# Attention and a cosine feed-forward: the output product of one more double tile done by seven block products

## The chip, the cores and the metric

The kernel runs on one core of one Trainium2 chip. The metric is the device time of one execution in microseconds (us). Before the change the median of three runs is 776.25 us (775.53 to 776.44).

The names of the engines in the profile: PE is TensorE's matmuls and PEld its weight loads, DVE is VectorE, ACT is ScalarE, POOL is GpSimd, SP is the queue that issues the DMAs.

## The reference

Attention within chunks of 64 positions, then a feed-forward layer with h·cos(h) between its two products, in fp32:

```python
scores = matmul(q_c, k_c^T) / sqrt(64)           # chunks of 64 of a sequence of 576; 8 batches, 8 heads
attn = softmax(scores); out = matmul(attn, v_c)
x = out.transpose(0, 2, 1, 3).reshape(4608, 512) # tokens by model width
h = x @ w_in                                     # w_in 512 x 2048
g = h * cos(h)
return g @ w_out                                 # w_out 2048 x 512
```

## The kernel before

Accuracy of fp32 is kept by splitting every operand into a high and a low fp32r part; a product is then three matmuls: high by high, high by low, low by high. In the profile the parts of g are `g_hi` and `g_lo`.

The 4608 tokens make 9 tiles of 512. Tiles 0 and 1 go first, alone. The other seven are handled in units: unit 0 is tile 2, unit 1 tiles 3 and 4, unit 2 tiles 5 and 6, unit 3 tiles 7 and 8. Attention of a later tile runs beside the feed-forward layer of an earlier unit.

**The hidden product** of a double tile is done by seven block products instead of eight (Strassen's scheme in Winograd's form): two halves of the tokens (the two tiles) by two halves of the hidden features. For each of eight pairs k of feature blocks there are seven products of six 128x512 matmuls (L324); sums of blocks of w_in are streamed from HBM. VectorE and ScalarE combine the seven results into four blocks of h (L969 copies, L972 additions) and make g out of each by four steps: an activation (`whole`, L975), `turn` (L978), an activation with the sine (`sine`, L982), and a multiplication (`times`, L985). Then g is split: a cast to g_hi (L339 on VectorE, L341 on ScalarE) and a subtraction to g_lo (L345 on VectorE or GpSimd).

**The output product** has two forms.

- Plain, `wide_pair` (L1610), in units 1 and 2: for each feature block of 128 and each 128 tokens three matmuls of 128x512. The first tile of the unit is multiplied at once, the g of the second tile is stored to the HBM tensor `gathered`, read back by `second_tile` (L1717) after the last pair, split and multiplied.
- By blocks, `block_pair` (L1775) and `block_products` (L1925), in unit 3: again seven products instead of eight, of 128x256 matmuls, over halves of the features, of the tokens and of the output columns. P1 and P2 take blocks of g as they are and run inside the pairs. For the other five, VectorE or GpSimd makes sums Z1 to Z4 of blocks of g (128x256 each, L345); these and the block Z22 are stored to the HBM tensor `sums` (L1897, L1899), and come back after the last pair, are split and multiplied with differences of w_out. Those differences are made by `differences_of_w` (L1690) during unit 1, stored to the HBM tensor `diffs` (L1711), loaded and split.

**Rooms.** Inside `block_pair` the four blocks of g of a pair lie in rooms in SBUF that the next pair takes again. In the last unit (`ends`) there are two rooms for each half of a pair (K_ROOMS, taken in turn: `twice = 2`), in another unit one (U_ROOM, T_ROOM: `twice = 1`). The first activation of a later pair, `w1`, waits for everything that reads the room (`k_users`, L1845, L1905): the store of Z22, the four sums and the split. In the last unit that is the pair before last, in another unit the pair before. The rooms of Z1 to Z4 (`q_room`, L1915) are the tiles of q and k in the last unit, else a tile of g, `half1` and the room `ds_room(1)`.

**What sets the order.** Every piece of work is appended with its engine and its dependences; then two tables decide. `RANK` gives each piece its place in one order, and so its place in its engine's queue; `ELSEWHERE` lists the pieces that run on their other engine (a split or a sum on GpSimd instead of VectorE). Engines work their queues strictly in order.

Of the kernel before, what the change touches and what calls it, by code (L numbers as in the profile page):

```python
# [289 lines left out]
def attention_then_cos_ffn(ctx: ExitStack, tc, qT, kT, v, w_in, w_out, out, wide):  # L290
# [593 lines left out]
    UNITS = 1 + (NT - FAST) // 2  # L884
# [133 lines left out]
    def out_part(t, fc, sub, half=None):  # L1018
# [15 lines left out]
        matmul(o, g_lo[:, ss], w_hi, start=False, stop=last, **on)  # L1034

    KK = NPAIR // 2
    BLOCKED = range(UNITS - 1, UNITS)
    ROWS, COLS = 2, HALF
    Z22, Z1, Z2, Z3, Z4 = range(5)
    V1, V3, V2, V4 = range(4)  # L1040
# [1456 lines left out]
```

## Time and profile before

| what | value |
|---|---|
| median of 3 runs | 776.25 us |
| the profiled execution | 775.76 us |
| its span | 774.1 us |
| TensorE matmul busy | 761.9 us, 98% |
| VectorE busy | 646.1 us, 83% |
| ScalarE busy | 444.6 us, 57% |
| GpSimd busy | 290.2 us, 37% |
| DMA, mean | 229 GB/s, 66.8% of 16 engines |

The profiled execution is one run; its span is the stretch from the first to the last recorded instruction, 1.66 us shorter than its device time. TensorE works nearly the whole span at a granted clock of 0.999 of full speed, so a reader looks for what shortens its work, and for what makes it wait.

The stages, as the timeline shows them: unit 2 (its pairs and its output product) from 457 to 621 us, the pairs of unit 3 from 621 to 707 us, the five products of unit 3 with the last results from 707 us on.

### The profile page before, as it was taken

Reading aid. Unit: us, or ns where it says so; the run is one execution under the profiler, and the core shown is the slowest. Engines: PE = TensorE matmul, PEld = TensorE weight load, DVE = VectorE, ACT = ScalarE, POOL = GpSimd, SP = SyncE. Lnnn points to the kernel's source line nnn. Section 1 sums busy time; section 2 is a strip of 40 time slices with the busy share of each in tenths; the row PEclk is TensorE's granted clock in tenths of the full one; section 3 lists DMA queues with packets and bytes.
Section 4 is the critical chain, followed back from the end, with each engine's and each line's share of the span. In section 5 each row is a group of like instructions: output and inputs, shape, how many; then the busy total and the mean of one; then the engine's idle time right before and its main releaser. Section 6 shows DMA issues by size and latency. Waiting matters only on the chain.

```text
span 774.1 us, 16060 instructions
## 1 busy us (share of the span) xinstructions
PE 761.9 (98%) x6100; PEld 676.2 (87%) x6100; DVE 646.1 (83%) x1100; ACT 444.6 (57%) x814; POOL 290.2 (37%) x261
## 2 busy tenths in 40 slices
PE   7999999999999999999999999999999999999997
PEld 6888888888999988888888888888888889989997
DVE  5997998889899987896899888777898667999983
ACT  6997885456884467555642445555443455556631
POOL 2442235968541344562521621201102027454144
PEclk9999999999999999999999999999999999999999
DMA  9995530389969645868674753757544376999973
GB/s 340 401 409 198 177 110 1 124 270 357 377 195 313 194 170 202 260 223 298 224 256 126 256 150 127 257 179 268 178 136 137 116 238 215 325 300 334 337 270 110
DMA packets 95756, 177.21 MB, mean 229 GB/s; under 512 B 9152, under 2 KB 39872, under 8 KB 95680
## 3 DMA queue, kind: packets, MB, share of 16 engines
q1 hardware_dynamic: 95680, 176.20, 66.8%
q8 instruction: 48, 0.79, 0.4%
q14 instruction: 28, 0.23, 0.1%
HBM read 127.93 MB, written 48.23 MB: 228 GB/s over the span
## 4 chain that ended last, share of the span: by engine, by line
PE 90%; DVE 4%; DMA 3%; POOL 1%; issue 1%; ACT 0%; SPq 0%; DVEq 0%; ACTq 0%
PE acc L324 41%; PE h L324 36%; PE a L324 13%; DVE g_lo L345 1%; DMA vt<-in_v_dram 1%; DMA w_in<-sums 1%; DMA sums<-qt 1%; POOL g_lo L345 1%; DMA kt<-in_kT_dram 1%; DVE g_hi L339 0%; DMA w_in<-diffs 0%; PE a L1207 0%; DVE x L345 0%; SPq L321 0%; DVE w_in L972 0%
## 5 line engine op out<-in xcount | busy, mean ns | idle before, releaser
L324 PE MATMUL acc<-w_out,g_hi 128*128 128x512 f32 (+1 forms) x976 | 278.3, 369 | 0.0
L324 PE MATMUL h<-x,w_in 128*128 128x512 f32 (+1 forms) x960 | 225.9, 364 | 0.0
L324 PEld LDWEIGHTS acc<-w_out,g_hi 128*128 128x128 f32 x976 | 178.1, 189 | 23.4 <-DVE w L339 0.7
L324 PEld LDWEIGHTS h<-x,w_in 128*128 128x128 f32 x960 | 171.2, 189 | 22.2
L324 PE MATMUL acc<-w_out,g_lo 128*128 128x512 f32 (+1 forms) x488 | 179.1, 367 | 0.0
L345 POOL TENSOR_TENSOR g_lo<-g,g_hi 128x512 fp32r<-128x512 f32 x38 | 53.2, 1400 | 193.2 <-ACT g_hi L341 97.9
L324 PEld LDWEIGHTS acc<-w_out,g_lo 128*128 128x128 f32 x488 | 92.4, 189 | 11.6
L324 PE MATMUL h<-w_in,w_in 128*128 128x512 f32 (+1 forms) x384 | 98.1, 354 | 0.5 <-DVE w_in L972 0.5
L324 PEld LDWEIGHTS h<-w_in,w_in 128*128 128x128 f32 x384 | 65.8, 190 | 8.7 <-DVE w_in L972 0.7
L982 ACT ACTIVATE w_in<-w_in 128x512 f32<-128x512 f32 x64 | 39.5, 628 | 18.8 <-DVE w_in L978 18.8
L341 ACT CAST g_hi<-g 128x512 fp32r<-128x512 f32 x52 | 32.0, 615 | 28.9 <-PE acc L324 8.5
L324 PE MATMUL a<-w_in,w_in 128*128 128x512 f32 (+1 forms) x204 | 42.5, 348 | 0.0
L345 DVE TENSOR_TENSOR g_lo<-g,g_hi 128x512 fp32r<-128x512 f32 x51 | 38.8, 761 | 3.2 <-ACT g_hi L341 2.5
L324 PE MATMUL a<-x,w_in 128*128 128x512 f32 (+1 forms) x192 | 41.2, 353 | 0.0
L345 POOL TENSOR_TENSOR g_lo<-w_in,g_hi 128x512 fp32r<-128x512 f32 x14 | 22.8, 1632 | 44.0 <-ACT g_hi L341 22.5
L324 PEld LDWEIGHTS a<-w_in,w_in 128*128 128x128 f32 x204 | 34.5, 190 | 4.0
L324 PEld LDWEIGHTS a<-x,w_in 128*128 128x128 f32 x192 | 33.2, 190 | 4.0
L969 ACT COPY a<-h 128x512 f32<-128x512 f32 x28 | 16.0, 571 | 33.5 <-PE h L324 31.0
L341 ACT CAST g_hi<-w_in 128x512 fp32r<-128x512 f32 x30 | 18.5, 619 | 26.1 <-PE acc L324 12.3
L345 DVE TENSOR_TENSOR g_lo<-w_in,g_hi 128x512 fp32r<-128x512 f32 x32 | 28.9, 916 | 5.2 <-ACT g_hi L341 4.9
L969 ACT COPY h<-h 128x512 f32<-128x512 f32 x28 | 16.0, 570 | 29.3 <-PE h L324 24.5
L725 ACT ACTIVATE g<-h 128x512 int32<-128x512 f32 x32 | 19.1, 596 | 23.4 <-PE h L324 20.7
(295 smaller groups left out, 1523.4 us busy)
## 6 DMA issues: line engine op xcount, KB each, us to landing
w_in<-combo SPq DMA_DIRECT2D x84, 512.0 KB, 4.8
combo<-w_in SPq DMA_DIRECT2D x56, 256.0 KB, 4.3
w_in<-combo SPq DMA_DIRECT2D x56, 256.0 KB, 5.3
qt<-in_qT_dram SPq DMA_DIRECT2D x36, 256.0 KB, 5.6
kt<-in_kT_dram SPq DMA_DIRECT2D x36, 256.0 KB, 5.6
w_in<-in_w_in_dram SPq DMA_DIRECT2D x16, 512.0 KB, 9.7
w_out<-in_w_out_dram SPq DMA_DIRECT2D x16, 512.0 KB, 9.9
gathered<-w_in SPq DMA_DIRECT2D x32, 256.0 KB, 3.1
```

The lines of the kernel that those rows point to most:

```text
L324: kept(nc.tensor.matmul(*args, **kw))
L341: kept(nc.scalar.copy(out=out, in_=in_))
L345: kept(eng.tensor_tensor(out, a, b, op=op))
L725: lambda: kept(nc.scalar.activation(n, h, AF.Identity, bias=0.25, scale=0.5 / math.pi)),
L969: kept(nc.scalar.copy(out=out, in_=in_))
L982: kept(nc.scalar.activation(g, g, AF.Sin, bias=0.5 * math.pi))
```

## The change

One number is changed in the code: the units whose output product goes by blocks start one earlier. The tables RANK (3206 numbers before, 3453 after) and ELSEWHERE are written anew for the whole kernel; of RANK two lines are shown.

```diff
 RANK = (
-    26, 32, 38, 44, 47, 37, 13, 56, 59, 64, 63, 53, 73, 78, 83, 75, 72, 81, 86, 90, 88, 79, 94, 98, 101, 99, 105,
...
+    3168, 3295, 3305, 3235, 3311, 3316, 3318, 3326, 3327, 3339, 3350, 3335, 3130, 3264, 3334, 3274, 3328, 3331,
...
-    BLOCKED = range(UNITS - 1, UNITS)
+    BLOCKED = range(UNITS - 2, UNITS)
```

So unit 2 (tiles 5 and 6) goes through `block_pair` and `block_products`, with `ends` false: one room a half, and the other rooms for the sums. The line that makes the differences of w_out, `if u == UNITS - 3` (L2431), is the same in both kernels. Lines of the changed kernel below the tables have numbers 15 higher.

Counted over the whole program, TensorE loses 384 matmuls of 128x512 and gets 672 of 128x256. VectorE gets 53 instructions more, ScalarE 39, GpSimd 49. The DMAs go from 574 to 654: 32 transfers of `gathered` fall away, 40 stores and 40 loads of `sums` and 16 loads of `diffs` are added, and results go out in more, smaller pieces.

TensorE's queue in a pair of unit 2 before: plain output products (`acc<-w_out,g_hi` and `g_lo`), and the start of a hidden block product (`h<-w_in,w_in`).

```order
L324 MATMUL acc_5902<-w_out_1122,g_hi 128x512 x2
L324 MATMUL acc_5902<-w_out_1122,g_lo 128x512
L324 MATMUL acc_5914<-w_out_997,g_hi 128x512 x2
L324 MATMUL acc_5914<-w_out_997,g_lo 128x512
L324 MATMUL h<-w_in_5449,w_in_6207 128x512
L324 MATMUL h<-w_in_5612,w_in_6207 128x512
L324 MATMUL h<-w_in_5449,w_in_6207 128x512 x2
L324 MATMUL h<-w_in_5612,w_in_6207 128x512
```

The same place of the changed kernel:

```order
L339 MATMUL acc_5932<-w_out_1033,g_hi 128x256 x2
L339 MATMUL acc_5932<-w_out_1033,g_lo 128x256
L339 MATMUL acc_5941<-w_out_1087,g_hi 128x256 x2
L339 MATMUL acc_5941<-w_out_1087,g_lo 128x256
L339 MATMUL acc_5941<-w_out_1087,g_hi 128x256 x2
L339 MATMUL acc_5941<-w_out_1087,g_lo 128x256
L339 MATMUL acc_5969<-w_out_1033,g_hi 128x256 x2
L339 MATMUL acc_5969<-w_out_1033,g_lo 128x256
L339 MATMUL acc_5932<-w_out_1033,g_hi 128x256 x2
L339 MATMUL acc_5932<-w_out_1033,g_lo 128x256
L339 MATMUL h<-w_in_5454,w_in_6289 128x512
```

The output matmuls of a pair are half as wide and belong to P1 and P2 alone; the rest of the output product stands in one run after the last pair.

VectorE's queue in a pair of unit 2 before, from a step of g to the next pair's additions (`L972`); the multiplications L985 end a block of g.

```order
L978 SCALAR_TENSOR_TENSOR g<-g,w_in_6149 128x512
L345 TENSOR_TENSOR g_lo<-g,g_hi 128x512
L985 TENSOR_TENSOR g<-w_in_6149,g 128x512
L339 CAST g_hi<-g 128x512
L642 STREAM_TRANSPOSE e_5754<-e_5792 32x8x32
L972 TENSOR_TENSOR w_in_6257<-a_6236,w_in_3870 128x512
L972 TENSOR_TENSOR w_in_6257<-h,w_in_3870 128x512
L978 SCALAR_TENSOR_TENSOR g<-g,h 128x512
L978 SCALAR_TENSOR_TENSOR g<-g,w_in_6257 128x512
```

And of the changed kernel, from the multiplication that ends the second block in one room (`w_in_6324`) to the first step in the next pair's block, which lies in the same room (`w_in_6541`); `g` and `w_in_3888` with 128x256 are the sums Z.

```order
L1000 TENSOR_TENSOR w_in_6324<-w_in_6344,w_in_6324 128x512
L1000 TENSOR_TENSOR w_in_6376<-w_in_6344,w_in_6376 128x512
L354 COPY e_5793<-a_6432 128x8x64
L354 COPY e_5793<-h 128x8x64
L360 TENSOR_TENSOR g<-g,w_in_6324 128x256
L360 TENSOR_TENSOR w_in_3888<-w_in_6376 128x256
L360 TENSOR_TENSOR g<-w_in_6324 128x256
L354 CAST g_hi<-w_in_6376 128x512
L354 COPY e_5752<-a_6389 128x8x64
L993 SCALAR_TENSOR_TENSOR w_in_6541<-w_in_6541,h 128x512
```

The sums stand between the steps of g, and between a block's last step and the next use of its room there are eight other instructions.

## Rows read from the trace of the kernel before

**Rows 1.** The page: the span, and each engine's busy time (part 1).

```profile
span 774.1 us, 16060 instructions
...
PE 761.9 (98%) x6100; PEld 676.2 (87%) x6100; DVE 646.1 (83%) x1100; ACT 444.6 (57%) x814; POOL 290.2 (37%) x261
```

**Rows 2.** Busy time by stretch, core 0; the head line names the columns.

```profile
core 0: us, PE busy (x) PEld busy (x) DVE busy (x) ACT busy (x) POOL busy (x), PEclk, DMA share, GB/s
457.00:621.00 164.00, 164.00 (x1232) 143.35 (x1231) 129.65 (x230) 80.41 (x133) 22.55 (x18) 1.00 0.52 176
621.00:707.00 86.00, 85.47 (x466) 76.43 (x465) 70.55 (x113) 47.88 (x84) 41.03 (x42) 1.00 0.85 277
707.00:747.00 40.00, 39.31 (x335) 38.21 (x335) 38.06 (x65) 21.63 (x39) 12.12 (x7) 1.00 0.98 331
...
260.00:280.00 20.00, 20.00 (x132) 18.61 (x131) 19.64 (x28) 11.75 (x23) 10.40 (x7) 1.00 0.73 235
```

**Rows 3.** The chain of waits, from 568 us: start, length, engine, what, line, instructions.

```profile
568.46 5.18 PE acc L324 x24
...
741.21 5.21 POOL g_lo L345
...
747.85 10.72 PE a L324 x96
```

**Rows 4.** Groups by line, VectorE, 621 to 707 us: busy us, mean ns, idle.

```profile
L978 DVE SCALAR_TENSOR_TENSOR w_in<-w_in,w_in 128x512 f32<-128x512 int32 x13 | 9.9, 772 | 0.3
...
L985 DVE TENSOR_TENSOR w_in<-w_in,w_in 128x512 f32<-128x512 f32 x13 | 9.5, 734 | 2.7 <-ACT w_in L982 2.6
...
L345 DVE TENSOR_TENSOR g_lo<-w_in,g_hi 128x512 fp32r<-128x512 f32 x8 | 9.3, 1192 | 1.3 <-ACT g_hi L341 1.3
...
L345 DVE TENSOR_TENSOR qt<-w_in 128x256 f32<-128x256 f32 x7 | 4.5, 647 | 0.0
...
L345 DVE TENSOR_TENSOR kt<-w_in 128x256 f32<-128x256 f32 x6 | 3.3, 544 | 0.0
...
L345 DVE TENSOR_TENSOR qt<-w_in,qt 128x256 f32<-128x256 f32 x2 | 0.8, 418 | 0.0
...
L345 DVE TENSOR_TENSOR g_lo<-g,g_hi 128x512 fp32r<-128x512 f32 x1 | 0.7, 684 | 0.0
```

**Rows 5.** The same view, GpSimd, 621 to 707 us.

```profile
L345 POOL TENSOR_TENSOR g_lo<-w_in,g_hi 128x512 fp32r<-128x512 f32 x6 | 8.7, 1450 | 6.6 <-DVE g_hi L339 6.6
...
L345 POOL TENSOR_TENSOR qt<-w_in 128x256 f32<-128x256 f32 x7 | 6.3, 904 | 11.9 <-DVE w_in L985 11.9
```

**Rows 6.** Timeline of VectorE: start, length, instruction; two stretches.

```profile
658.54 0.42 DVE L345 TENSOR_TENSOR kt<-w_in 128x256 f32<-128x256 f32 x1
658.88 1.23 DVE L978 SCALAR_TENSOR_TENSOR w_in<-w_in,w_in 128x512 f32<-128x512 int32 x1
...
709.32 0.68 DVE L345 TENSOR_TENSOR w_in<-w_in 128x512 fp32r<-128x512 f32 x1
709.92 0.68 DVE L345 TENSOR_TENSOR g_lo<-g,g_hi 128x512 fp32r<-128x512 f32 x1
```

**Rows 7.** Groups by line, VectorE, the whole span: transposes of the attention.

```profile
L642 DVE STREAM_TRANSPOSE pts<-e 32x256 f32<-32x256 f32 x40 | 17.0, 432 | 0.9
```

**Rows 8.** Line L1897, the 128 KB stores of unit 3's block of g.

```profile
L1897 SPq DMA_DIRECT2D sums<-w_in x16: 320/398/1027, 620.0 to 716.1; - x16
...
DMA to landing us min/median/max: 1.7/4.8/7.1
```

**Rows 9.** The DMA view: issues, KB each, median us to landing.

```profile
gathered<-w_in SPq DMA_DIRECT2D x32, 256.0 KB, 3.1
```

**Rows 10.** Timeline of TensorE at a late operand in unit 3's products.

```profile
737.63 0.38 PE L324 MATMUL acc<-x,g_lo 128*128 128x256 f32 x1 [0.24 <-DVE g_lo L345]
```

**Rows 11.** Tile diffs: its stores, with first and last start.

```profile
L1711 SPq DMA_DIRECT2D diffs<-w_in x16: 370/382/1457, 306.7 to 398.0; - x16
```

383 rows, old and new, of tables (ELSEWHERE, RANK) are left out of this document.

## The prediction

> **What bounds the kernel now.** I read the page first: TensorE's matmuls are busy 761.9 of 774.1 us, 98%, VectorE 83%, GpSimd 37% [rows 1]. So the time is TensorE's work, and a change must take work from it or make it wait. The table by stretch says where it waits: in unit 2, from 457 to 621 us, not at all (164.00 of 164.00) with VectorE busy 129.65 and DMAs at a share of 0.52; in unit 3, which already does its output product by blocks, 0.53 us in the 86 us of pairs and 0.69 in the 40 us of products [rows 2]. Unit 3 is therefore the nearest picture of what unit 2 becomes. What differs is shown nowhere in the trace: unit 2 also carries the attention of tile 7, and its pairs have one room for g where unit 3 has two. The chain of waits gives the prices of the two matmuls: 24 of 128x512 in 5.18 us, 0.2158 us each, and 96 of 128x256 in 10.72 us, 0.1117 each [rows 3]. The narrow one costs a little over half.
>
> **TensorE's work.** 384 x 0.2158 = 82.9 us goes, 672 x 0.1117 = 75.0 us comes: -7.8 us. That is the only term that can make the kernel faster, and as TensorE never waits in unit 2, it counts in full if nothing else is late.
>
> **VectorE in the pairs.** I add up the changed queue between the first addition of pair 0 and that of pair 7. TensorE's matmuls there make 97.1 us by the two prices above. VectorE has 163 instructions. They follow one another closer than their length: 0.60 us from start to start where the row says 0.68, 0.34 where it says 0.42 [rows 6]. So 108 on 512 elements x 0.60 = 64.8, 31 transposes x 0.43 [rows 7] = 13.3, 16 on 256 elements or casts x 0.34 = 5.4, 8 tiny ones x 0.2 = 1.6 (my estimate): 85.1 us. To this comes what GpSimd does to VectorE. In unit 3's pairs VectorE's instructions with two operands in SBUF are longer than the 684 ns (512 elements) and 418 ns (256 elements) of undisturbed ones: 13 x 88, 13 x 50, 8 x 508, 7 x 229 and 6 x 126 ns, 8.2 us together [rows 4], beside 41.03 us of GpSimd's work [rows 2], 0.20 us for each. In the changed queue GpSimd has 42 sums x 0.904 and 13 splits x 1.450 [rows 5], 56.8 us, in these pairs: +11.4. VectorE then needs 96.5 of 97.1 us. TensorE kept its pace with VectorE at 19.64 of 20 us, 98% [rows 2], so 96.5 / 0.98 = 98.5, +1.4 us.
>
> **The single room.** The first activation in a room waits for the store of Z22 of the pair before. In the changed queue of VectorE the time from the end of a block's last step to the first step in its room's next block is, by the same durations, 11.97, 6.82, 5.40, 4.72, 3.76, 9.14 and 6.49 us over the seven pairs; the excerpt of the changed queue shows the one of 3.76. In it must fit the issue (0.4, rounded to 0.5) and landing of the store and the activation with its signals (0.7, my estimate). Landing took 4.8 us in the median and 7.1 at most in unit 3, at a DMA share of 0.85 [rows 2, 8], and 3.1 in the stretches of `gathered`, at 0.52 and with twice the bytes [rows 2, 9]. At 3.1 only one pair is late, by 0.5 us; at 4.8 three are, 0.6 + 1.3 + 2.2 = 4.1; at 7.1 five are, some 14 us. The changed pairs move about what unit 3's do (277 GB/s x 86 us = 23.8 MB) in 97 us, 246 GB/s, so I put the share at 0.76 and the landing at 4.3 us: 2.6 us late. Part of this VectorE makes up, as the other pairs have 2 to 7 us to spare, and part is the same idle time as the 2% above. For the pairs I take +2.5 us together, between 0.5 and 7 (4.1 and twice 1.4).
>
> **The products of unit 2.** TensorE's work there is 67.5 us. VectorE has 122 instructions: 86 x 0.60 + 17 x 0.43 + 19 x 0.34 = 65.4, and 11 splits on GpSimd x 1.450 x 0.20 = 3.2, 68.6 us. 68.6 / 0.98 = 70.0, +2.5. Beside it operands come late as in unit 3, where a matmul waited 0.24 us for a split [rows 10] and a split on GpSimd of 5.21 us stood in the chain [rows 3]; that stretch lost 0.69 us in 40, so 1.2 in 67.5. They overlap with the first; I take +3.0, between 1.2 (VectorE ahead by its pieces done early) and 7.4 (both, and as much again, since here every split starts from a load). The loads themselves: 40 of `sums`, 16 of `diffs`, the streamed w_in, q, k, v and the results make some 20 MB in 67.5 us, 300 GB/s, where unit 3's products had 331 at a share of 0.98 [rows 2]; they fit, with little to spare. The differences are no new work: their stores ran from 306.7 to 398.0 us [rows 11], before unit 2 begins, and the order has them at the same place.
>
> **The rest.** ScalarE gets 39 instructions of about 0.6 us, 23 us on an engine with 57% [rows 1]: hidden by VectorE's queue, which is longer; in the products it has some 48 us of 67.5. SP issues 80 more DMAs, 0.4 us each [rows 8], 32 us over two stretches of 165 us: hidden, though a store now queues behind the streams, which is in the 0.5 us above. Unit 3's pairs and products keep their code. The order before unit 2 is rewritten too, with 12 VectorE instructions more ahead of unit 0's first addition; TensorE's idle time outside the stretches above is 12.2 - 1.2 = 11.0 us, nearly all at the start and the end, and I let it move by 0, at most 1.5 either way.
>
> **The sum.** -7.8 + 2.5 + 3.0 + 0 = -2.3 us on the profiled execution's 775.76 (its span 774.1 and 1.66 around it), 773.45. That execution lies 0.49 us under the median of the runs, so 773.9 us.
>
> **Rivals.**
>
> A. The whole saving arrives. For it: TensorE lost nothing with VectorE at 98%, and unit 3 does the same work with 0.53 us lost [rows 2]. Against it: there VectorE had 18% to spare. It needs landings near 3.1 us. -7.8 + 0.5 = -7.3 to -7.8: 768.5 to 769.0.
>
> B. VectorE takes TensorE's place as the bound and the time stays. VectorE's 96.5 + 68.6 = 165.1 us stand against 172.4 (164.6 and the 7.8 saved): the change is worth nothing from the point where VectorE can't be kept busy more than 95.8%. The trace has 38.06 of 40 with a loss and 19.64 of 20 without [rows 2], one on either side: 776.2, give or take 1.5.
>
> C. Slower, by the single room. If the landings of Z22 are 5.9 us, halfway between median and maximum of unit 3 [rows 8], the same list gives 0.3 + 1.7 + 2.4 + 3.3 + 0.6 = 8.3 us; with the products' 3.0 that is +3.5: 779.7. By itself it turns the sign from about 5.1 us of landing, where the list gives 5 us. For it speaks the DMA share, against it that unit 2 moves its bytes in more time.
>
> D. Slower, by GpSimd standing in VectorE's way more than in unit 3. If every us of GpSimd blocks VectorE for the share of its time that goes to instructions with two SBUF operands, 0.33 in the pairs and 0.67 in the products as I count the queue, VectorE needs 85.1 + 18.7 = 103.8 and 65.4 + 10.7 = 76.1, 179.9 us in place of 164.6: -7.8 + 15.3 = +7.5, 783.7. Against it: unit 3's 0.20 is what that overlap did cost, with a like mixture. The Trainium skill, "SBUF — State Buffer", section "Who interferes with whom", has this as a rule: VectorE and GpSimd share one pair of ports as an exclusive lock, so that "the other **fully blocks** (not throttle)". The trace agrees that splits beside GpSimd take 1192 ns in place of 684 [rows 4]; it does not show each of them blocked, so I keep the measured rate in the sum.
>
> **How the numbers follow.** What a measurement can tell from no change is 0.2%, 1.55 us. Forecast (part of the saving, 770 to 774.7): 0.42. A: 0.13. B (774.7 to 777.8): 0.22. C: 0.14, D: 0.09. So faster 0.55, same 0.22, slower 0.23. The forecast's own range is 770 to 774.7; to hold 8 in 10 it reaches down to A and up over C: 768.4 to 780.5.
>
> **What would show it.** In the changed profile: 672 more matmuls at 0.11 us and 384 fewer at 0.216; a stretch of some 100 us of pairs in unit 2 with TensorE idle 2 to 3 us in it, released by VectorE's L987; VectorE at 95% or more there; activations L990 of a first block waiting on DMA of `sums` in two or three pairs (C: in most of them, DMA as releaser, over 1 us each). In the products of unit 2 TensorE's gaps end with g_lo on VectorE or GpSimd. If VectorE's two-operand instructions average above 900 ns there, D is right. The prediction is wrong if TensorE loses time in unit 3 or before 457 us, which I cost at nothing, or if unit 2's loads land late enough that TensorE waits on a DMA.

## The result and the profile after

The changed kernel takes 786.41 us, median of 4 runs (785.79 to 787.93), the kernel before 776.35 us beside it: a ratio of 1.0127, with a 95% interval of 1.0112 to 1.0142. It is 10 us slower; the forecast was 773.9 us and its range ended at 780.5. (The section on the change says 3206 numbers for the table RANK before; it has 3216. It says 39 more instructions for ScalarE; the two profiles below differ by 53, of which 47 are casts, and by 31.8 us of ScalarE's time, where the prediction counted 23.)

The page of the changed kernel, span and part 1, answers to [rows 1]:

```profile
span 784.1 us, 16988 instructions
...
PE 760.1 (97%) x6388; PEld 678.0 (86%) x6388; DVE 678.0 (86%) x1153; ACT 476.4 (61%) x867; POOL 330.7 (42%) x310
```

The number of matmuls rose by 288 as counted, but their busy time fell by 1.8 us only and the time in which TensorE does nothing rose from 12.2 to 24.0 us. Measured from start to start (median 216 ns for 128x512, 112 for 128x256, and 109 and 7 for the small ones, which are the same in both kernels), TensorE's work fell by 7.7 us, as predicted, from 725.6 to 717.9. What grew is the rest of the time between its first and its last matmul, the time lost, from 40.0 to 58.1 us. Part of it counts as busy: after a wait the first group of matmuls is about 0.10 us longer, as in this row of TensorE's timeline in a pair of unit 2, where six take 1.56 us in place of 1.46 (start, length, instruction, the idle time before it and who ended it):

```profile
489.59 1.56 PE L339 MATMUL h<-w_in,w_in 128*128 128x512 f32 x6 [0.60 <-DVE w_in L987]
```

The table by stretch of the changed kernel (to be read beside [rows 2]; in this kernel unit 2's pairs run from about 452 to 558 us, and its products to 628, where unit 3's pairs take over):

```profile
core 0: us, PE busy (x) PEld busy (x) DVE busy (x) ACT busy (x) POOL busy (x), PEclk, DMA share, GB/s
0.00:452.00 452.00, 444.17 (x3842) 389.60 (x3843) 392.68 (x672) 285.21 (x537) 211.15 (x194) 1.00 0.68 237
452.00:556.00 104.00, 100.20 (x873) 86.82 (x872) 92.79 (x161) 62.48 (x102) 49.62 (x54) 1.00 0.74 246
556.00:600.00 44.00, 38.58 (x316) 36.57 (x316) 39.90 (x71) 28.64 (x51) 12.02 (x9) 1.00 1.02 358
600.00:640.00 40.00, 38.10 (x402) 35.98 (x401) 36.24 (x63) 21.63 (x39) 5.39 (x4) 1.00 0.51 168
```

Four things are to be seen. TensorE, which never waited in unit 2 before, is idle 3.8 us in the pairs, 5.4 in the first 44 us of the products and 1.9 around the step to unit 3. VectorE is busy 92.79 us of 104 in the pairs, 89%, which is less than the 95% that the prediction named. The DMAs are at a share of 1.02, busy all the time, and at 358 GB/s from 556 to 600 us, and at half of that afterwards. And before 452 us TensorE is busy 444.17 us, where the kernel before has

```profile
0.00:452.00 452.00, 445.54 (x3851) 391.61 (x3852) 391.67 (x673) 285.12 (x541) 203.95 (x187) 1.00 0.68 235
```

TensorE's waits from 452 to 636 us (in all, times, longest):

```profile
engine line waited for: us in total, times, longest us
PE h L339 <- DVE w_in L987: 2.2, 3, 1.4
PE h L339 <- DVE w_in L1000: 1.4, 2, 0.9
PE acc L339 <- ACT half L356: 1.2, 1, 1.2
PE a L339 <- DVE g_lo L360: 1.1, 2, 0.8
PE a L339 <- ACT g_hi L356: 1.0, 2, 0.6
PE h L339 <- ACT h L984: 0.7, 1, 0.7
PE acc L339 <- ACT w L356: 0.7, 1, 0.7
PE h L339 <- ACT e L356: 0.7, 1, 0.7
```

They have many releasers and none stands out: VectorE's additions (L987) and multiplications (L1000) in the pairs, casts of loaded sums and copies that empty banks of PSUM, TensorE's result memory, by ScalarE (L356) in the products. So the causes have to be left out one after the other.

### The profile page after: what moved, and what is told of

Same layout as the page of the kernel before. It is cut to its first block, busy times and chain, and to the rows that moved or that the text cites. A ratio compares the mean times of both kernels' runs of the same rounds, so it can differ in the third digit from the quotient of the medians.

```text
span 784.1 us, 16988 instructions
## 1 busy us (share of the span) xinstructions
PE 760.1 (97%) x6388; PEld 678.0 (86%) x6388; DVE 678.0 (86%) x1153; ACT 476.4 (61%) x867; POOL 330.7 (42%) x310
## 4 chain that ended last, share of the span: by engine, by line
PE 85%; DMA 6%; DVE 5%; ACT 2%; issue 1%; SPq 1%; DVEq 0%; ACTq 0%
PE acc L339 37%; PE h L339 32%; PE a L339 15%; DMA w_in<-combo 2%; DVE w_in L993 1%; DVE w_in L1000 1%; DMA x<-diffs 1%; SPq L336 1%; DMA qt<-in_qT_dram 1%; DMA x<-sums 1%; DMA w_in<-sums 1%; DVE w_in L987 1%; DMA kt<-in_kT_dram 1%; DVE g L360 0%; ACT w_in L990 0%
## 5 line engine op out<-in xcount | busy, mean ns | idle before, releaser
L339 PE MATMUL acc<-w_out,g_hi 128*128 128x512 f32 (+1 forms) x848 | 224.6, 352 | 0.0
L339 PEld LDWEIGHTS acc<-w_out,g_hi 128*128 128x128 f32 x848 | 150.6, 190 | 17.0
L339 PE MATMUL acc<-w_out,g_lo 128*128 128x512 f32 (+1 forms) x424 | 148.3, 350 | 0.0
L360 POOL TENSOR_TENSOR g_lo<-g,g_hi 128x512 fp32r<-128x512 f32 x33 | 44.4, 1345 | 123.2 <-ACT g_hi L356 81.2
L339 PEld LDWEIGHTS acc<-w_out,g_lo 128*128 128x128 f32 x424 | 80.5, 190 | 8.1
L360 POOL TENSOR_TENSOR g_lo<-w_in,g_hi 128x512 fp32r<-128x512 f32 x18 | 25.3, 1412 | 57.9 <-PE acc L339 24.7
L356 ACT CAST g_hi<-w_in 128x512 fp32r<-128x512 f32 x51 | 31.4, 620 | 23.3 <-PE acc L339 11.0
L360 DVE TENSOR_TENSOR g_lo<-w_in,g_hi 128x512 fp32r<-128x512 f32 x52 | 38.7, 753 | 6.0 <-ACT g_hi L356 5.4
L990 ACT ACTIVATE w_in<-w_in 128x512 int32<-128x512 f32 x40 | 25.0, 629 | 25.6 <-DVE w_in L987 24.8
L990 ACT ACTIVATE w_in<-h 128x512 int32<-128x512 f32 x40 | 23.9, 598 | 23.1 <-PE h L339 20.2
L993 DVE SCALAR_TENSOR_TENSOR w_in<-w_in,h 128x512 f32<-128x512 int32 x40 | 27.4, 685 | 11.5 <-ACT w_in L990 11.0
L360 POOL TENSOR_TENSOR w_in<-w_in 128x256 f32<-128x256 f32 (+1 forms) x31 | 27.3, 895 | 20.8 <-DMA x<-sums 12.5
L1000 DVE TENSOR_TENSOR w_in<-w_in,w_in 128x512 f32<-128x512 f32 x40 | 30.4, 763 | 2.5 <-ACT w_in L997 2.3
```

Source lines behind the costliest of these rows:

```text
L339: kept(nc.tensor.matmul(*args, **kw))
L356: kept(nc.scalar.copy(out=out, in_=in_))
L360: kept(eng.tensor_tensor(out, a, b, op=op))
L990: kept(nc.scalar.activation(g.bitcast(I32), h, AF.Identity, bias=0.25, scale=0.5 / math.pi))
L993: kept(nc.vector.scalar_tensor_tensor(g, g.bitcast(I32), -2.0 * math.pi, h, op0=ALU.mult, op1=ALU.add))
L1000: kept(nc.vector.tensor_tensor(g, h, g, op=ALU.mult))
```

## The experiments

All times are medians of 4 to 10 runs, each kernel beside runs of the kernel before on the same chip (its medians lay between 775.7 and 776.6 us). The text of each expectation says what the kernel leaves out or takes from elsewhere; the code is abridged. Prices below are differences of these medians; one of under about 1.5 us is not clear of noise.

**Without the sums**

```diff
 def take(by, o, a, b, op, i=i, new=False):
+    if u == UNITS - 2:
+        return
...
-    in_=v["q", i][n - 1]
+    in_=w_parts["out", 0][0] if u == UNITS - 2 else v["q", i][n - 1]
```

> The changed kernel without the sums Z1 to Z4 of unit 2's blocks of g (64 instructions on VectorE and GpSimd); their stores send a resident block of w_out instead, so every transfer stays. Theory: in the pairs of unit 2 TensorE waits because VectorE's queue is full. Then the waits of TensorE for VectorE there go, some 6 of the 7 us that the pairs lose against before: about 780.5 us. Rival: the pairs wait for stores (the single room of g) or for the order in which attention stands; all that is still there, so 785.5 to 786.5.

Measured: 783.48 us, 2.9 less than the changed kernel (ratio to before 1.0092, 1.0077 to 1.0108). From 484 to 526 us, in four of the pairs, the changed kernel first and this one behind it:

```profile
484.00:526.00 42.00, 39.95 (x331) 34.63 (x330) 38.68 (x68) 22.93 (x42) 21.54 (x24) 1.00 0.83 272
```

```profile
484.00:526.00 42.00, 40.80 (x339) 36.17 (x339) 33.32 (x59) 23.89 (x42) 5.42 (x5) 1.00 0.92 299
```

VectorE falls from 92% to 79% busy, GpSimd from 21.54 to 5.42 us, and the waits for L987 inside the pairs go; but TensorE gets only 0.85 of its 2.05 idle us back. So the sums in these two engines' queues were a cause, for 2.9 us, and not the main one.

**Products from resident operands, and both edits**

```diff
     for sub in range(2):
         pairs = ...
+        if u == UNITS - 2:
+            pairs = [[w_at(2 * (2 * kk + n), half, part) for half in range(2) for part in range(2)] for n in range(2)]
```

> The changed kernel with the five products of unit 2 taking their operands from resident blocks of w_out; all loads, splits and stores still run. Theory: TensorE waits there for operands that are loaded and split late, 5 to 6 us of it: about 780.5 us. Rival: it waits for PSUM banks to be emptied by ScalarE and for the handover to unit 3, which stay: 785 us or more.

> Both edits: no sums in unit 2's pairs, and its products from resident operands. Theory: the two losses are separate and add up, 11 to 12 us: 774 to 775.5 us, at last under the kernel before by about the early part's and the handover's loss short of the 7.8 us of matmuls. Rival: one loss hides behind the other, or turns up in unit 3: 778 us or more.

Measured: 784.98 us (1.0113, 1.0098 to 1.0128) and 783.68 us (1.0091, 1.0074 to 1.0109). Freeing TensorE of its late operands gave 1.4 us, which is not clear of noise, and nothing on top of the missing sums. Both expectations of the theory failed. The timeline of ScalarE in the kernel with both edits shows why:

```profile
570.71 1.30 ACT L356 CAST g_hi<-x 128x512 fp32r<-128x512 f32 x2 [1.45 <-DMA x<-sums]
...
573.34 0.62 ACT L356 CAST g_hi<-x 128x512 fp32r<-128x512 f32 x1 [1.33 <-DMA x<-sums]
...
574.90 0.58 ACT L356 COPY w<-acc 128x512 f32<-128x512 f32 x1
```

The casts of loaded sums wait for their DMAs though no matmul reads them any more, and the copy that empties a bank of PSUM (`w<-acc`) stands behind them in the queue; TensorE, with its operands at hand, waited 3.23 us for that copy:

```profile
575.53 1.86 PE L339 MATMUL acc<-w_out 128*128 128x256 f32 x7 [3.23 <-ACT w L356]
```

In the changed kernel the same is seen at 592 us: a cast waits 1.94 us for a load of differences, the copy of a bank stands behind it in ScalarE's queue, and TensorE waits 1.24 us for that copy.

```profile
591.62 0.62 ACT L356 CAST x<-x 128x512 fp32r<-128x512 f32 x1 [1.94 <-DMA x<-diffs]
592.15 0.58 ACT L356 COPY half<-acc 128x512 f32<-128x512 f32 x1
```

```profile
592.78 0.49 PE L339 MATMUL acc<-w_in,g_hi 128*128 128x256 f32 x2 [1.24 <-ACT half L356]
```

So a late load holds up what stands behind it in ScalarE's queue, and to take one of the waiters away shows nothing.

**The early order**

The first 1749 pieces get the places and engines that they have in the kernel before (tables alone).

> The changed kernel with the first 1749 pieces in the order, and on the engines, that they have in the kernel before; unit 2 and unit 3 as changed. Theory: the rewritten order of the early part costs the 1.8 us wait of TensorE near 187 us: about 784.6 us. Rival: it costs nothing in the end, 786 to 786.5.

Measured: 787.53 us (1.0145, 1.013 to 1.016). TensorE's wait of 1.8 us near 187 us went, and two waits of 2.0 us together came in unit 1, between 419 and 426 us, where the old order meets the new; TensorE is busy 444.20 us before 452 us, as in the changed kernel. This one doesn't settle what the early order costs.

**Without the operand path of the products, in whole and in parts**

```diff
-    load(r[n], sums_g[u, i, kk][:, j])
+    if u != UNITS - 2: load(r[n], sums_g[u, i, kk][:, j])     # and the casts and subtractions after it
-    load(lo, diffs[kk][:, j])
+    if u != UNITS - 2: load(lo, diffs[kk][:, j])              # and the casts and subtractions after it
```

The first of the next kernels has both edits, the second that of the differences alone, the third only the casts and subtractions of the differences left out, and the fourth is like the third with loads of `[:, :16]`.

> The changed kernel; in unit 2's five products all loads of sums and differences and all splits of them are left out, the matmuls take resident blocks of w_out. Theory: with resident operands but loads and splits kept only 1.4 us came back because ScalarE's queue (casts behind loads, ahead of the copies that empty the banks) kept TensorE; without them the bank copies come in time: 780 to 781 us. Rival: banks and handover have waits of their own: 784 us or more.

> The changed kernel; in unit 2's products the 16 loads of differences of w_out and their 32 splits are left out (those operands resident), the loads and splits of the sums stay. Theory: the products start in a stretch where the DMAs are at a share of 1.03, so 4 MB less and 32 splits less give about half of what leaving out the whole path gives: 783 us. Rival: the sums' own loads decide: 785.5 us or more.

> The changed kernel; in unit 2's products the 32 splits of the differences are left out and their matmuls take resident blocks, the 16 loads stay. Leaving out loads and splits gave 5 us. Theory (the 32 instructions in the full queues of ScalarE and VectorE are what costs): 782 us. Rival (the 4 MB in a stretch where the DMAs are at a share of 1.02): 785 to 786 us.

> As the run without the splits of the differences, but the 16 loads of differences in unit 2's products bring 16 of 512 columns each: the same 16 issues with the same waits in SP's queue, 8 KB each instead of 256. Theory (the 4 MB where the DMAs are at a share of 1.02 cost 3.5 us): 781.5 us, as without these loads. Rival (their issues and waits hold up the loads behind them in SP's queue): 784 to 785 us.

Measured: 778.73 us (1.0027, 1.0011 to 1.0043), 781.44 (1.0063, 1.0047 to 1.008), 784.90 (1.0099, 1.0067 to 1.013) and 781.18 (1.0073, 1.0054 to 1.0091). The stretch from 556 to 600 us of each, in that order:

```profile
556.00:600.00 44.00, 42.75 (x367) 42.10 (x366) 21.41 (x43) 11.55 (x20) 4.86 (x5) 1.00 0.39 126
```

```profile
556.00:600.00 44.00, 42.09 (x360) 41.09 (x360) 36.47 (x67) 22.19 (x39) 4.81 (x5) 1.00 0.91 308
```

```profile
556.00:600.00 44.00, 40.20 (x324) 38.76 (x324) 32.68 (x60) 21.48 (x37) 5.26 (x5) 0.96 1.01 359
```

```profile
556.00:600.00 44.00, 42.06 (x355) 40.81 (x354) 36.34 (x66) 22.05 (x38) 5.52 (x5) 1.00 0.93 304
```

The whole path costs 7.7 us, more than expected. The differences have 5.0 of it. Their 32 splits are worth 1.5, not clear of noise, so the theory of the third run fell: with the loads left in, the DMAs stay at 1.01 and TensorE is idle 3.8 us. With the same 16 issues and waits but 4 MB less to bring, the share is 0.93, TensorE is idle 1.9, and the time is that without the differences. So the bytes cost, and not the issues: 3.7 us between the two medians. Beside each one's own runs of the kernel before the difference is smaller, 1.0099 to 1.0073 or 2.0 us, and the intervals overlap; but the slowest run without the bytes (781.59 us) is faster than the fastest with them (783.23). What is left of the path, 2.7 us, is the sums' own loads and splits.

**Both losses left out**

> The changed kernel without unit 2's sums and without the loads and splits of its products. Theory: the two add up, 2.9 + 5.5: 778 us; what is then left over the 768.6 us that the matmuls alone would give is the waits of attention and of copies in the pairs (4 us), the handover to unit 3 (2.6) and the early part (1.8). Rival: something else replaces them: 781 us or more.

Measured: 776.78 us (1.0008, 0.999 to 1.0027), a little better than expected. With the sums gone and the loads and splits of the products too, the kernel is level with the one before: some 8 us above the 768.6 that the matmuls alone would give. (The stores of the blocks are still there.) Its pairs, products and step to unit 3:

```profile
452.00:556.00 104.00, 100.79 (x886) 88.56 (x885) 86.51 (x152) 63.05 (x104) 16.61 (x13) 1.00 0.76 252
556.00:600.00 44.00, 43.30 (x382) 42.95 (x381) 16.89 (x32) 10.39 (x18) 1.28 (x1) 1.00 0.31 102
600.00:640.00 40.00, 37.91 (x369) 34.61 (x369) 26.10 (x43) 18.36 (x34) 5.30 (x5) 1.00 0.31 99
```

TensorE still loses 3.2 us in the pairs, where no sum runs, and 2.1 around the step to unit 3. On top come the 0.10 us that it loses after each wait, and one wait of 1.75 us in unit 3 for a load of sums of w_in.

**The kernel before with narrower matmuls in unit 2**

```diff
+if t in (FAST + 3, FAST + 4) and not first and not last:      # second run: tile FAST + 3 alone,
+    o, w_hi, w_lo = o[:, :440], w_hi[:, :220], w_lo[:, :220]  # 344 columns, the first product too
 matmul(o, g_hi[:, ss], w_lo, ...)
 matmul(o, g_lo[:, ss], w_hi, ...)
```

> The kernel before, unit 2 as it was (plain output product), but 224 of its output matmuls in unit 2 are 440 of 512 columns wide: 6.8 us less work for TensorE and nothing else changed. Theory (what the blocks add or the order makes is what costs, TensorE's work by itself could go): about 769.5 us. Rival (unit 2's plain matmuls are the cover of other waits, so that any work taken from there comes back as waits): 773 us or more.

> The kernel before, with 168 output matmuls of tile 5, all inside unit 2's pairs, 344 of 512 columns wide: TensorE's work in these pairs falls by 11.9 us, about as much as the change takes from them (106.4 to 94.3 us), and nothing else changes. Theory (cover: with so little work of its own in a pair TensorE waits for attention's banks, copies and additions): some 5 us of it come back, about 769.5 us. Rival (the pairs have room for it; the waits of the changed kernel come of how its pairs and attention are set in order): all of it arrives, about 764.5 us.

Measured: 769.86 us (0.9916, 0.9899 to 0.9932), so 6.8 us less, all of what was taken; and 767.20 us (0.9876, 0.9852 to 0.9901), 9.0 less of 11.9 (by the interval 7.7 to 11.5). From 452 to 556 us the two kernels show

```profile
452.00:556.00 104.00, 104.00 (x849) 93.02 (x848) 82.79 (x149) 57.55 (x92) 16.42 (x13) 1.00 0.62 208
```

```profile
452.00:556.00 104.00, 103.11 (x873) 91.87 (x872) 86.02 (x155) 59.77 (x98) 16.67 (x13) 1.00 0.62 213
```

With work taken thinly from the whole unit TensorE keeps its 104 us; with as much taken from the pairs as the change takes, 2.9 us come back, less than the 5 expected: 0.9 of them idle in the pairs, the others lost after each wait and in waits for splits where the second tile's product begins. Among them are waits at the same place of the attention as in the changed kernel, the matmuls that need a bank which VectorE still reads (here, and then in the changed kernel, with the multiplication that it waits for):

```profile
518.39 0.27 PE L325 MATMUL h<-e,qt 64*64 64x64 f32 x2 [0.47 <-DVE w_in L986]
```

```profile
518.43 0.27 PE L339 MATMUL h<-e,qt 64*64 64x64 f32 x2 [0.51 <-DVE w_in L1000]
```

```profile
517.68 0.69 DVE L1000 TENSOR_TENSOR w_in<-h,w_in 128x512 f32<-128x512 f32 x1
```

## Why the prediction was wrong

**The sum's first term held.** 7.7 us of matmuls went, against 7.8.

**Where the time went, by stage.** Counted in the profiled executions, as TensorE's time from each matmul's start to the next beyond the median of its shape, the changed kernel loses 9.3 us more than the one before in the pairs of unit 2, 5.3 in its products, 2.9 at the step to unit 3 (the first 78 hidden matmuls there) and 1.9 ahead of unit 2, and 1.3 less in the rest of unit 3: 18.1 in all, where the prediction had 2.5, 3.0, 0, 0 and 0. In the kernel with neither sums nor operand path the same stages give 6.2, -0.1, 2.9, 1.6 and -1.0, and in the kernel before with 344 columns the pairs give 3.2.

**The products were mis-sized: +3.0 predicted, 7.7 measured.** The step that failed is "some 20 MB in 67.5 us, 300 GB/s [...] they fit, with little to spare". It is an average over a stretch that isn't even: 358 GB/s at a share of 1.02 in the first 44 us, 168 at 0.51 after that. The chain of waits runs through loads there (start, length):

```profile
557.31 5.06 DMA x<-sums
...
574.30 4.87 DMA w_in<-sums
...
579.24 6.47 DMA w_in<-combo
...
585.72 5.88 DMA x<-diffs
```

The prediction counted operands that come late at the rate of unit 3 (1.2 us) and let VectorE's queue set the rest. In fact the loads set it, the 4 MB of differences alone 2.0 to 3.7 us, and through ScalarE's queue they hold up the bank copies too. One load in the chain, `w_in<-combo`, is no operand of the products: it streams sums of w_in for unit 3 through the same DMAs. What that stream costs here no run tested.

**The pairs: +2.5 predicted, 9.3 measured.** The sums cost 2.9 us, about what the prediction took for VectorE's load and the single room together; that is luck, since VectorE came to 89% and not 95%, and the store that the room was to wait for held up nothing (below). The step that failed is that TensorE's saved work "counts in full if nothing else is late", with no price on what else was. The plain matmuls of unit 2 were what TensorE did while attention's banks, ScalarE's copies and the additions came round; the change takes 12 us of them out of the pairs (106.4 to 94.3 us from start to start) and puts them in one run behind. I gave that cover no price. By itself it is worth 2.9 us (0.4 to 4.2 by the interval), as the kernel with 344 columns shows; with the order of the changed kernel TensorE is still 3.2 us idle there when sums and operand path are gone. What that order, the smaller matmuls and the blocks' stores have of the difference was not taken apart.

**The step to unit 3, at nothing.** "Unit 3's pairs and products keep their code" is true and beside the point: the output product of unit 2 used to lie between unit 3's first hidden products, and now all but 12 of its matmuls are over when they begin. TensorE's timeline at the same place, before and after:

```profile
614.55 1.46 PE L324 MATMUL a<-x,w_in 128*128 128x512 f32 x6
615.85 0.59 PE L324 MATMUL acc<-w_out,g_hi 128*128 128x512 f32 x2
...
618.22 0.38 PE L324 MATMUL acc<-w_out,g_lo 128*128 128x512 f32 x1
618.43 1.46 PE L324 MATMUL h<-w_in,w_in 128*128 128x512 f32 x6
```

```profile
633.74 1.46 PE L339 MATMUL a<-x,w_in 128*128 128x512 f32 x6
636.74 1.53 PE L339 MATMUL h<-w_in,w_in 128*128 128x512 f32 x6 [1.54 <-ACT w_in L990]
```

Before, 12 output matmuls (2.6 us) fill the time; after, TensorE waits 1.54 us for an activation, with nothing else to do. From 600 to 640 us it is idle 1.9 us (the last row of the table). All changed kernels here have this loss, and none was built to take it away.

**Rival C, the single room, did not come.** What ScalarE waited for before the first activations and the others of L990 from 452 to 560 us:

```profile
its engine sat idle before it (us, times) until:
  DVE w_in L987: 8.0, 8
  PE h L339: 6.6, 8
  DVE g L360: 1.6, 1
  POOL g L360: 0.6, 1
```

No store is among them, so the 2.6 us late that the prediction took were not there. What the room did wait for are sums that read it (`g` L360), 2.2 us of ScalarE's time.

**Rival D, more contention than in unit 3, did not come either.** The prediction's sign for it was an average above 900 ns for VectorE's two-operand instructions. In the pairs of unit 2 the splits alone pass that, 906 ns, where unit 3 had 1192 [rows 4]; with the multiplications (722) and the turns (684) of the same size the average is some 760. In all, these instructions and the sums took 5.9 us more than undisturbed ones, beside 49.62 us of GpSimd's work: 0.12 us for each, where the prediction took 0.20 from unit 3.

```profile
L360 DVE TENSOR_TENSOR g_lo<-w_in,g_hi 128x512 fp32r<-128x512 f32 x7 | 6.3, 906 | 0.9 <-ACT g_hi L356 0.9
```

The Trainium skill's rule ("SBUF — State Buffer", "Who interferes with whom") is that the loser of the lock is blocked in full. The prediction said that the trace does not show each instruction blocked; read one by one, the rows do. A sum on VectorE starts while a split runs on GpSimd, which ends at 522.10, and it takes 1.25 us, until 0.28 after that end:

```profile
521.13 1.25 DVE L360 TENSOR_TENSOR g<-g,w_in 128x256 f32<-128x256 f32 x1
```

```profile
520.82 1.28 POOL L360 TENSOR_TENSOR g_lo<-w_in,g_hi 128x512 fp32r<-128x512 f32 x1 [0.21 <-ACT g_hi L356]
```

Of the 58 instructions of L360 on VectorE in the changed kernel that start while one of GpSimd has over 0.17 us left, 57 end 0.28 us (256 elements) or 0.55 us (512) after GpSimd's, within 0.04 us; those that find GpSimd idle, or that it joins later, take their 0.42 or 0.69. So what an overlap costs is the rest of the GpSimd instruction that is running, and the means of a group only say how often that happened.

**Rival B was nearest, with the wrong limit and too low a price.** VectorE's queue did cost TensorE time in the pairs, but the kernel did not stop at level with the one before, since three losses that the prediction counted little or at nothing came beside it. In the sum: -7.7 of matmuls, +7.7 of the products' operands, +2.0 of sums (2.9 by themselves, 2.0 between the kernels without the operand path and without both), and some 8 that the kernel without either still has over its matmuls. The trace of that kernel, which loses 9.5 us more than the one before in its profiled execution, has them in the pairs (6.2), at the step to unit 3 (2.9) and ahead of unit 2 (1.6, with the wait near 187 us), less 1.0 in the rest of unit 3. Why they are there was shown by a run only for the cover, with 2.9 us; the rest is read from the traces and not shown.

No version that beats both kernels came out of this: without sums and operand path the changed order is only level with the one before.

## What to carry to other kernels

Matmuls that depend on little are cover: TensorE does them while other engines' results come. Before they are cut or bundled behind a loop, look at what stands between the places where the loop must wait. Add up the bytes over the first tens of microseconds of a new stage, not over the whole of it: here a stage that loaded its operands from HBM took 358 GB/s at its start and 168 later. And when an engine's queue is in order, a late load delays what has nothing to do with it, so an experiment has to leave out the whole path, not one of its readers.

## What the runs showed of the hardware

In four of the kernels, after waits of TensorE of 1.4 to 3.2 us between 567 and 578 us, the granted clock fell for a few microseconds, as in that without splits of the differences (two stretches of 4 us; PEclk is the third number from the end):

```profile
572.00:576.00 4.00, 2.31 (x16) 1.93 (x15) 1.35 (x2) 1.56 (x3) 0.00 (x0) 0.94 1.07 387
...
576.00:580.00 4.00, 4.00 (x26) 4.00 (x25) 2.40 (x5) 1.89 (x4) 0.00 (x0) 0.63 1.00 322
```

0.63 is some 3 us of the four at 1.2 GHz in place of 2.4. The runs of this kernel with and without it differ by no more than runs do (784.73 us at a mean clock of 1.0, 783.23 and 785.64 at 0.997), so no conclusion above rests on it.

A wait of TensorE cost about 0.10 us beyond its length, in nearly all of some 20 waits over 0.1 us from 452 to 640 us: the matmul behind the first one starts that much later.
